# Pairs 7 and 8 transposed by DMA, early T work, and a DMA exchange in a fused attention and feed-forward kernel

## The chip, the cores and the metric

The kernel runs on one core of one Trainium2 chip. The metric is device microseconds of one execution; of several executions the median counts. A profile of one execution stands beside them. TensorE is PE in the profile (its weight loads PEld), VectorE is DVE, ScalarE is ACT, GpSimd is POOL, SyncE is SP.

## The reference

```python
def _attn_ref(q, k, v):                      # (8, 8, 1152, 64) each
    q_pool = q.reshape(B, H, S // 2, 2, D).mean(axis=3)      # 576 pooled queries a head
    scores = 1.0 / np.sqrt(D) * np.matmul(q_pool, k.transpose(0, 1, 3, 2))
    ...                                                      # softmax over the 1152 keys
    return np.matmul(attn, v)

def _moe_ref(x, w1, w2, w3, w_out):          # x (4608, 512): heads side by side
    a = x @ w1                               # (512, 1024)
    b = x @ w2
    h = a * b @ w3                           # (1024, 1024)
    return h @ w_out                         # (1024, 512)
```

The arithmetic is in 16-bit floats with sums in 32 bits; the result is 32-bit.

## The kernel before, in words

**Work.** The 64 heads are taken as 32 pairs; pair P is heads 2P and 2P+1, four pairs make a batch element. A pair's scores are 9 blocks of keys by 576 queries, and the two heads stand in the two 64-row halves of PE. The scores of all pairs form one stream that is cut in 324 chunks of 512 columns, so a pair is 10.1 chunks, and a boundary between pairs falls inside a chunk. `scores(c)` (L303) computes a chunk, `expo(c)` (L309) is ACT's exponential into the ring `er`, which holds 1.78 pairs. `attend(P, us)` (L312) multiplies the exponentials with the values (tile `po`; u is the head), `normalize` (L351) divides and sends the result, transposed by a DMA on SP, into `xT`. The last 64 queries of each head are the remainders: they go through `rems` by DMA into `xR` (the second half of the batches into a view of `wosb`), and `cross` (L378) copies each 64-row half of it into the other half.

**Feed-forward.** The product w3 @ w_out is formed once as `T16`: `w3_transpose(c)` (L476) transposes a block of w3 on PE (tile `w3t`, L493) and multiplies it with w_out (`pT`, L505), eight blocks in all. `add_batch(b)` then makes gates (`pg`, L546: x @ w1 and x @ w2 for 256 tokens, DVE copies one half and multiplies) and rows (`pp`, L570: gate times `T16`, then the store). w1 and w2 are loaded once and needed with their 64-row halves exchanged as well; `swap_halves` (L411) does that with a matmul by a swapped identity (`sw`, L419) and a copy.

**Preparation of a pair.** Keys and queries must be transposed. Pairs 1 to 8 (below `NPE`) take `prep_stage` and `prep_pe`: DVE copies the keys into `kc` and adds neighbouring queries into `qp` (`pool_q`, L138; for pairs 7 and 8 POOL makes the key copy), PE transposes (`t`, L271), DVE moves the results to `kT` and `qT` (L265, L261). From pair 9 on `prep_dma` (L158) does it: POOL copies the keys, adds the queries and copies the values, and two DMA transposes on SP (`turn_k` L168, `turn_q` L174) fill `kT` and `qT`. `turn_k` also has POOL wait for `kT` and then issue the loads of pair P + 5.

**The order.** The program is written out by a planner while it is built. It keeps a planned time for each PE half (`clock`), one for DVE (`vec`), and planned landings; its zero lies at the first scores, which start at 8.2 us in the profile. For each chunk it asks when the exponentials let the next scores go (`due`), and fills the time until then with one `step` of prepared work: first the queue `prep` (transposes), then `ffn` (T blocks, later the batches, in order). `LEAD` limits how far half 0 may run ahead of half 1 in `ffn`. `bursts` says at which chunk each pair's attention is multiplied (`BEHIND`, and `APART` for the distance of the two heads, J for both at once). `events`, `STAGE`, `PREP` and `turns` are in pairs of progress: `at = c * 512 / 5184`. `early` gives the chunk from which a T block may be queued. Each engine runs its instructions in the order written, so POOL's loads, copies and sums are one queue, and SP's transposes, exchanges and stores another.

Of the kernel before, what the change touches and what calls it, by code (L numbers as in the profile page):

```python
# [23 lines left out]
def kernel(  # L24
# [19 lines left out]
    SCL = 16.0  # L44
    NPE = 9
    T_SC, T_ACT, T_EXP, T_SEM, T_PV, LEAD = 0.225, 0.93, 1.05, 0.25, (1.78, 1.4), 2.53
    SCALE = 0.5 * float(D) ** -0.5
# [136 lines left out]
    def prep_stage(P):  # L184

        def copy_k(eng=nc.vector):
            eng.tensor_copy(out=new_kc(P).rearrange("p j u d -> p u j d"), in_=kst.pop(P))
# [12 lines left out]
        jobs.append((560, pool, LANDED[P][1]))  # L200
# [110 lines left out]

    def attend(P, us):  # L312

        pos = []
        for u in us:
            n = take()
            po = bank("po", n)
            pos.append((n, po, u))
            for j in range(NJ):
                for i in range(4):  # L320
                    r = ((P * NJ + j) * SQ) % RING + 128 * i
                    nc.tensor.matmul(  # L322
                        po[:, VW * i:VW * i + D + 1], er[:, u, r:r + 128],
                        vts[P % 4][:, u, j, 0:D + 1],
                        start=(j == 0 and i == 0), stop=(j == NJ - 1 and i == 3),
                        skip_group_check=True)
            if u == 0:
                for j in range(NJ):
# [6 lines left out]
        at = max(clock[0], clock[1], exp_done[last_chunk(P)] + T_SEM, V_COPIED.get(P, 0.0))  # L335
        b, hp = divmod(P, 4)
        for i, (n, po, u) in enumerate(pos):
            at += T_PV[u] - (0.2 if i else 0.0)
            give(n, normalize(P, u, po, 5 - u, at))
        clock[:] = [at] * 2  # L340
        if 0 in us and b % 2 == 1:
# [36 lines left out]
    def cross():  # L378

        b, _ = crossing.pop(0)  # L380
        x = xR[b // 4]
        k = (b // 2) % 2
        for h in range(2):
            nc.vector.tensor_copy(out=x[64 * h:64 * h + 64, 2 - 2 * h, :, k],  # L384
                                  in_=x[64 - 64 * h:128 - 64 * h, 1, :, k])
            vector(128, 0.0)
        if k == 1:
            crossed[b // 4][0] = vec + T_SEM

# [10 lines left out]

    def load_ffn(h):
        cols = slice(512 * h, 512 * h + 512)
        for dst, src in ((w1sb, moe_w1), (w2sb, moe_w2)):
            nc.gpsimd.dma_start(out=dst[:, 0, :, cols],
                                in_=src.rearrange("(c p) f -> p c f", p=128)[:, :, cols])
            swaps[h].extend((dst, c, cols) for c in range(NC))

# [68 lines left out]
    def w3_transpose(c):  # L476
# [3 lines left out]
        left = [2]  # L480
        landed = 13.0

# [12 lines left out]
        for h in range(2):  # L495
            add(prep, Block("w3t", NF, (h,), lambda t, at, h=h: out(t, at, h), FP16),
                0.0285, [[W3_LANDED[c // 2]]], emit)

# [107 lines left out]
    def step(h):  # L606
# [3 lines left out]
        for q in (prep[h], ffn[h]):  # L610
# [5 lines left out]
            q.pop(0)  # L616
            clock[h] += cost
            if q is ffn[h]:
# [19 lines left out]
    def last_rows(places, lhsT):  # L638
# [18 lines left out]
    NCHUNK = NP * PAIR // CH  # L657

    load_q(0)
    load_k(0)  # L660
# [3 lines left out]
        base=0, channel_multiplier=1, pattern=[[-1, 128]])  # L664
    load_v(0)
    load_k(1)
    load_q(1)
    load_w3(0)
    load_w(wosb, moe_w_out)
    load(2)  # L670
    load_w3(1)
    load(3)
    load_w3(2)
    nc.gpsimd.tensor_copy(out=swap[:, 0:64], in_=ident[:, 64:128])
# [3 lines left out]

    def last_chunk(P):
        return -(-(P + 1) * PAIR // CH) - 1  # L680

    def copy_v_later(P):
        if P < 4:
            jobs.append((280, lambda: copy_v(P), 0.0))
# [7 lines left out]
    LANDED = {1: (3.1, 4.3), 2: (13.4, 15.1), 3: (20.9, 22.7), 4: (28.9, 30.4), 5: (36.9, 38.1),  # L692
              6: (47.2, 48.8), 7: (57.9, 59.2), 8: (62.5, 64.6)}
# [12 lines left out]
    bursts = []  # L706
    for P in range(NP):
        at = last_chunk(P) + int(BEHIND[P])
        if APART[P] == "J":
            bursts.append((at, P, (1, 0)))  # L710
        else:
            bursts += [(at, P, (1,)), (at + int(APART[P]), P, (0,))]
    bursts.sort()

# [10 lines left out]
    while c < NCHUNK or bursts or ffn[0] or ffn[1]:  # L725
        h = 0 if clock[0] <= clock[1] else 1
        if crossing and crossing[0][1] < clock[h]:
            cross()
        if bursts and (c > bursts[0][0] or c == NCHUNK) and len(spare) >= len(bursts[0][2]) and (
                spare[len(bursts[0][2]) - 1][0] < clock[h]) and (  # L730
                fresh or c > bursts[0][0] + 1 or c == NCHUNK):
            attend(*bursts.pop(0)[1:])
# [4 lines left out]
        if c >= NCHUNK or due(c) > clock[h]:  # L737
# [5 lines left out]
            if bursts and c > bursts[0][0] - 1:  # L743
                keep = len(bursts[0][2])
            if not step(h):
# [13 lines left out]
        for i in range(2):  # L759
            clock[i] += T_SC  # L760
        expo(c)
# [3 lines left out]
        if jobs:  # L765
            n, job, landed = jobs.pop(0)
            job()
            vector(n, landed)
        if staged < NPE and at >= STAGE.get(
                staged, staged - (0.95 if staged < 4 else 1.3)):  # L770
# [55 lines left out]
```

## Time and profile before

| | |
|---|---|
| Runs | 418.47 us median of 3 (417.0 to 418.74) |
| Profiled execution | 415.05 us; span of its instructions 413.3 us |
| Granted clock of TensorE | 0.999 |
| PE, PEld busy | 395.1 us, 318.6 us |
| DVE, ACT, POOL busy | 224.4, 323.7, 191.7 us |
| DMA | 58.98 MB in 94217 packets |

Busy is time in which an engine had an instruction running. The ends of matmuls are modelled, so a high share of PE does not say that it ran at its peak. A stretch A:B is in microseconds from the start of the span. In a group's line the figures are busy time, mean nanoseconds of one instruction, and the idle time before them; in a DMA's line the last figure is the median time from issue to landing.

### The profile page before, as it was taken

The page shows a single profiled execution, that of the slowest core. Times are in us where ns is not written, and L with a number is a line of the kernel's source. Part 1 is how long each engine was busy: PE and PEld are TensorE (multiplying, and loading weights), DVE is VectorE, ACT ScalarE, POOL GpSimd, SP SyncE. Part 2 cuts the span into 40 slices and gives each one's busy share as a digit, 9 for nine tenths or more (in the row PEclk, how much of TensorE's full clock was granted, in tenths as well). Part 3 has the DMA queues.
Part 4 walks back from the last instruction along what each step waited for, and adds up shares of the span by engine and source line. Part 5 has one row for each costly group of instructions (what it writes and reads, how often), then busy time and mean ns, then how long its engine had stood idle before and what let it go on. Part 6 is the DMA issues. An engine that isn't in the chain of part 4 may idle for free.

```text
span 413.3 us, 16876 instructions
## 1 busy us (share of the span) xinstructions
PE 395.1 (96%) x7410; PEld 318.6 (77%) x7410; DVE 224.4 (54%) x585; ACT 323.7 (78%) x369; POOL 191.7 (46%) x209
## 2 busy tenths in 40 slices
PE   3699999999999999999999999999999999999996
PEld 1376765858778887887798986799688888998883
DVE  2256678585545564654465653477556644653530
ACT  3978889987989988879887889888888889834432
POOL 8243345770666666655654666665659400000000
PEclk9999999999999999999999999999999999999999
DMA  8999999998999999999999999999996324102004
GB/s 123 201 207 206 203 205 206 187 179 131 142 159 193 146 148 150 210 134 132 185 173 135 143 144 159 199 169 140 139 175 144 44 61 126 29 19 103 2 14 142
DMA packets 94217, 58.98 MB, mean 143 GB/s; under 512 B 64832, under 2 KB 84544, under 8 KB 94144
## 3 DMA queue, kind: packets, MB, share of 16 engines
q0 software_dynamic: 26528, 33.56, 52.3%
q1 hardware_dynamic: 67456, 24.22, 33.9%
q8 instruction: 58, 0.95, 1.0%
q10 hardware_dynamic: 160, 0.13, 0.1%
q14 instruction: 15, 0.12, 0.1%
HBM read 67.11 MB, written 9.44 MB: 185 GB/s over the span
## 4 chain that ended last, share of the span: by engine, by line
PE 92%; ACT 2%; DVE 2%; DMA 1%; issue 1%; POOL 0%; DVEq 0%; POOLq 0%
PE pg L546 30%; PE psc L303 19%; PE po L322 18%; PE pp L570 15%; PE pT L505 3%; PE po L331 3%; ACT er L309 2%; DMA kst<-in_k_dram 1%; PE sw L419 1%; PE t L271 1%; DVE wosb L384 1%; PE w3t L493 1%; DVE qp L145 0%; PE pp L644 0%; DVE asb L525 0%
## 5 line engine op out<-in xcount | busy, mean ns | idle before, releaser
L309 ACT ACTIVATE er<-psc 128x1024 f16<-128x1024 f32 x324 | 303.6, 1047 | 50.4 <-PE psc L303 50.1
L303 PE MATMUL psc<-qT,kT 64*128 64x512 f16 (+7 forms) x1152 | 128.8, 290 | 4.3 <-ACT er L309 3.8
L546 PE MATMUL pg<-xT,w2sb 64*128 64x256 f16 x1024 | 126.6, 269 | 0.2 <-issue 0.2
L546 PE MATMUL pg<-xT,w1sb 64*128 64x256 f16 x1024 | 124.7, 269 | 0.0
L546 PEld LDWEIGHTS <-w2sb 64*128 64x128 f16 x1152 | 94.9, 94 | 8.2 <-issue 1.9
L546 PEld LDWEIGHTS <-w1sb 64*128 64x128 f16 x1152 | 94.4, 94 | 7.2
L570 PE MATMUL pp<-T,gT 64*128 64x512 f16 (+1 forms) x552 | 94.3, 376 | 1.3 <-DVE gT L538 0.7
L303 PEld LDWEIGHTS <-kT 64*128 64x128 f16 x1152 | 63.1, 95 | 30.5 <-issue 16.0
L322 PEld LDWEIGHTS <-er 128*128 128x128 f16 x2304 | 73.7, 98 | 11.2 <-issue 8.7
L322 PE MATMUL po<-vt,er 128*128 128x65 f16 x2304 | 79.6, 194 | 0.1
L538 DVE TENSOR_TENSOR gT<-pg,asb 128x256 f16<-128x256 f32 x144 | 64.1, 445 | 19.2 <-ACT asb L522 14.1
L525 DVE COPY asb<-pg 128x256 f32<-128x256 f32 x116 | 49.0, 423 | 33.7 <-PE pg L546 32.7
L145 POOL TENSOR_TENSOR qp<-qst 64x1152 f16<-64x1152 f16 x23 | 54.9, 2388 | 1.0
L570 PEld LDWEIGHTS <-gT 64*128 64x128 f16 (+1 forms) x552 | 40.8, 94 | 14.5 <-issue 1.3
L355 DVE RECIPROCAL rz<-po 128x4 f32<-128x4 f32 x64 | 12.1, 188 | 71.0 <-PE po L331 37.2
L170 POOL COPY seen<-kT 1x1 f16<-1x1 f16 x19 | 3.4, 179 | 83.5 <-DMA kT<-kc 83.5
L154 POOL COPY vt<-vst 128x1152 f16<-128x1152 f16 x28 | 32.3, 1155 | 5.5 <-issue 4.8
L125 POOL DMA_DIRECT2D vst<-in_v_dram x32 | 23.4, 731 | 16.4 <-DMA kst<-in_k_dram 5.7
L118 POOL DMA_DIRECT2D kst<-in_k_dram x33 | 24.0, 729 | 10.6 <-issue 3.0
L358 DVE TENSOR_TENSOR xn<-po,rz 128x256 f16<-128x256 f32 x64 | 27.2, 425 | 2.4 <-DVE rz L355 0.2
L163 POOL COPY kc<-kst 128x1152 f16<-128x1152 f16 x23 | 27.0, 1173 | 0.0
L522 ACT COPY asb<-pg 128x256 f32<-128x256 f32 x28 | 10.4, 373 | 19.0 <-PE pg L546 15.3
(66 smaller groups left out, 255.4 us busy)
## 6 DMA issues: line engine op xcount, KB each, us to landing
qst<-in_q_dram POOLq DMA_DIRECT2D x32, 288.0 KB, 6.3
vst<-in_v_dram POOLq DMA_DIRECT2D x32, 288.0 KB, 7.8
kst<-in_k_dram POOLq DMA_DIRECT2D x31, 288.0 KB, 5.3
out_dram<-osb SPq DMA_DIRECT2D x32, 256.0 KB, 3.9
w3h<-in_moe_w_dram POOLq DMA_DIRECT2D x4, 512.0 KB, 15.0
wosb<-in_moe_w_out_dram POOLq DMA_DIRECT2D x1, 1024.0 KB, 13.4
xT<-xn SPq DMA_TRANSPOSE x64, 5.4
w1sb<-in_moe_w_dram POOLq DMA_DIRECT2D x2, 512.0 KB, 14.8
```

Source lines behind the costliest of these rows:

```text
L118: nc.gpsimd.dma_start(out=kst[P][:, :, js[0]:js[1], :], in_=k[b, h0:h0 + 2].rearrange("u (p j) d -> p u j d", j=NJ)[:, :, js[0]:js[1], :])
L145: (eng or nc.vector).tensor_tensor(out=qps[pp][r].rearrange("p c u d -> p u c d"), in0=src[:, :, :, 0, :], in1=src[:, :, :, 1, :], op=ALU.add)
L154: (eng or nc.vector).tensor_copy(out=vts[P % 4][:, :, :, 0:D], in_=vst.pop(P))
L163: nc.gpsimd.tensor_copy(out=kc.rearrange("p j u d -> p u j d"), in_=kst.pop(P))
L303: nc.tensor.matmul(t[:, u, o:o + ln], kT[P][s, j, :], qv[s, f0:f0 + ln], start=True, stop=True)
L309: nc.scalar.activation(out=er[:, :, r:r + CH], in_=psc.pop(c), func=AF.Exp, bias=0.0, scale=SCALE)
L322: nc.tensor.matmul(po[:, VW * i:VW * i + D + 1], er[:, u, r:r + 128], vts[P % 4][:, u, j, 0:D + 1], start=(j == 0 and i == 0), stop=(j == ...
L358: nc.vector.tensor_tensor(out=xn, in0=acc[:, 0:4, 0:D], in1=rz[:, 0:4].to_broadcast([128, 4, D]), op=ALU.mult)
L525: nc.vector.tensor_copy(out=a, in_=t[:, 0:n])
L538: nc.vector.tensor_mul(out=g, in0=b, in1=a)
L546: nc.tensor.matmul(t[:, n * w:n * w + n], (w1sb, w2sb)[w][s, (m + h) % 2, m // 2, fs], x(h, s, m), start=start, stop=stop, skip_group_chec ...
L570: nc.tensor.matmul(t, g(s, i), T16[s, i, :], start=start, stop=stop, skip_group_check=True)
```

## The change

- `NPE` goes from 9 to 7: pairs 7 and 8 take `prep_dma`. Their value copies stay separate events, their turns come at P - 1.6 and P - 1.35, and they issue no loads. `PREP` has them at 4.7 and 5.75; a pair is only prepared after the pair before it (pair 6 at 4.94). The loads of pairs 9, 10 and 11 move from 4.75, 5.0, 5.95 to 5.2, 5.9, 6.1.
- `early` goes from chunks (14, 14, 19, 21, 26, 30, 39, 40) to (7, 7, 17, 18, 31, 41, 41, 43), and up to five blocks may be open instead of four.
- `cross` uses two DMAs on SP instead of two DVE copies; the plan lets the remainder's gates wait 6 us more, and delays the first exchange of each two by 6 us.
- The order of the loads is written as a list, and the planned landings `LANDS` are a formula over it. The order up to pair 8 is the same as before. The halves of w1 and w2 become swappable one by one, from planned 42.3 and 62.6 instead of 46.0 and 70.4.
- `LEAD` goes from 2.53 to 3.79; until the planned time `COLD` = 9 matmuls count double in the plan; the times in `STAGE` and `PREP`, `BEHIND` and `APART` are new.
- A burst may be cut into slices, and a T block may be transposed by DMA; `SLICES`, `W3_DMA` and the letter D leave both unused.

```diff
-    NPE = 9
-    T_SC, T_ACT, T_EXP, T_SEM, T_PV, LEAD = 0.225, 0.93, 1.05, 0.25, (1.78, 1.4), 2.53
+    NPE = 7
+    T_SC, T_ACT, T_EXP, T_SEM, T_PV, LEAD = 0.225, 0.93, 1.05, 0.25, (1.78, 1.4), 3.79
+    COLD = 9.0
...
         pool_q(P, nc.gpsimd)
-        copy_v(P, nc.gpsimd)
+        if P > 8:
+            copy_v(P, nc.gpsimd)
...
-            if P + 5 <= NP:
+            if P > 8 and P + 5 <= NP:
...
-        turns.extend([(P - 1.45, turn_k), (P - 1.2, turn_q)])
+        turns.extend([(P - (1.45 if P > 8 else 1.6), turn_k), (P - (1.2 if P > 8 else 1.35), turn_q)])
...
-        if P == 7:
-            copy_k(nc.gpsimd)
-            kc_done[P] = LANDED[P][0] + 9.0
-        elif P == 8:
-            copy_k(nc.gpsimd)
-            kc_done[P] = LANDED[P][0] + 10.0
-        else:
-            jobs.append((280, copy_k, LANDED[P][0]))
+        jobs.append((280, copy_k, LANDED[P][0]))
...
-                crossing.append((b, landed))
+                crossing.append((b, landed + (6.0 if b % 4 == 1 else 0.0)))
...
         for h in range(2):
-            nc.vector.tensor_copy(out=x[64 * h:64 * h + 64, 2 - 2 * h, :, k],
-                                  in_=x[64 - 64 * h:128 - 64 * h, 1, :, k])
-            vector(128, 0.0)
+            nc.sync.dma_start(out=x[64 * h:64 * h + 64, 2 - 2 * h, :, k],
+                              in_=x[64 - 64 * h:128 - 64 * h, 1, :, k])
         if k == 1:
-            crossed[b // 4][0] = vec + T_SEM
+            crossed[b // 4][0] = max(clock) + 6.0
...
-        return bool(swaps[half]) and max(clock) > WEIGHTS[half] and len(spare) >= free and (
+        if not swaps[half]:
+            return False
+        landed = LANDS[("f" if swaps[half][0][0] is w1sb else "g") + str(half)] + T_SEM
+        return max(clock) > max(WEIGHTS[half], landed) and len(spare) >= free and (
             spare[0][0] < min(clock))
...
-        landed = 13.0
+        landed = LANDS["wo"]
...
-            clock[h] += cost
+            clock[h] += cost * (2 if clock[h] < COLD else 1)
...
+    ORDER = ("v0 k1 q1 w0 wo k2 q2 v1 w1 k3 q3 v2 w2 k4 q4 v3 w3 k5 q5 v4 "
+             "f0 g0 k6 q6 v5 f1 g1 k7 q7 v6 k8 q8 v7").split()
+    mb, LANDS = 0.0, {}
+    for n in ORDER:
+        mb += {"w": 1.05, "f": 1.05, "g": 1.05}.get(n[0], 0.59) * (2 if n == "wo" else 1)
+        LANDS[n] = 0.3 + 2.38 * mb if mb < 5.51 else 13.4 + 2.74 * (mb - 5.51)
...
-    early = list(zip((14, 14, 19, 21, 26, 30, 39, 40), range(8)))
-    STAGE = {1: 0.39, 2: 1.2, 3: 2.0, 4: 3.02, 5: 4.2, 6: 4.94, 7: 5.15, 8: 6.95}
-    W3_LANDED = (7.1, 19.0, 27.6, 35.1)
+    early = list(zip((7, 7, 17, 18, 31, 41, 41, 43), range(8)))
+    STAGE = {1: 0.39, 2: 1.26, 3: 2.02, 4: 2.85, 5: 3.5, 6: 4.32, 7: 5.15, 8: 6.95}
+    W3_LANDED = [LANDS["w%d" % i] for i in range(4)]
...
-    PREP = {1: 0.67, 2: 1.38, 3: 1.9, 4: 3.2, 5: 4.43, 6: 5.41, 7: 5.72, 8: 7.49}
+    PREP = {1: -0.42, 2: 0.76, 3: 2.34, 4: 2.61, 5: 2.95, 6: 4.94, 7: 4.7, 8: 5.75}
     events = sorted(
-        [(0.0, 4, load), (0.0, 3, load_w3), (0.4, 5, load), (0.4, 0, load_ffn), (1.2, 6, load),
-         (1.2, 1, load_ffn), (2.3, 7, load), (4.0, 8, load), (4.75, 9, load), (5.0, 10, load),
-         (5.95, 11, load), (6.95, 12, load), (7.05, 13, load)]
-        + list(zip((1.97, 2.59, 3.9, 4.35, 5.1, 5.4, 6.1, 7.0), range(1, NPE),
-                   [copy_v_later] * NPE)), key=lambda e: e[0])
-    WEIGHTS = (46.0, 70.4)
+        list(zip((0.0,) * 4 + (0.4,) * 5 + (1.2,) * 5 + (2.3,) * 3 + (4.0,) * 3, ORDER[13:],
+                 [issue] * 20))
+        + [(5.2, 9, load), (5.9, 10, load), (6.1, 11, load), (6.95, 12, load), (7.05, 13, load)]
+        + list(zip((1.55, 2.95, 3.21, 4.35, 5.1, 5.4, 6.1, 7.0), range(1, 9),
+                   [copy_v_later] * 8)), key=lambda e: e[0])
+    WEIGHTS = (42.3, 62.6)
...
-    BEHIND = "22123222333244224212222222232434"
-    APART = "35J2144JJ42JJ1J2JJJJJ41J4J14J3JJ"
+    BEHIND = "22422222333442422221223242212432"
+    APART = "33344434J2J4JJJ221JJ36JJ3J3JJ4JJ"
...
-        elif early and c >= early[0][0] and len(w3T) < 4:
+        elif early and c >= early[0][0] and len(w3T) < 5 and (
+                early[0][1] < W3_DMA or W3_LANDED[early[0][1] // 2] < clock[0] + 1.0):
```

More of the change, by code (lines that the diff above doesn't have):

```diff
@@ L310, in expo, with attend @@
                              bias=0.0, scale=SCALE)
-    def attend(P, us):
+    held = {}
+    def attend(P, us, js=range(NJ)):
         pos = []
         for u in us:
-            n = take()
-            po = bank("po", n)
+            if js[0] == 0:
+                n = take()
+                held[P, u] = n, bank("po", n)
+            n, po = held[P, u]
             pos.append((n, po, u))
-            for j in range(NJ):
+            for j in js:
                 for i in range(4):
@@ L327, in attend @@
             if u == 0:
-                for j in range(NJ):
+                for j in js:
                     r = ((P * NJ + j) * SQ) % RING + 512
@@ L334, in attend @@
                             skip_group_check=True)
-        at = max(clock[0], clock[1], exp_done[last_chunk(P)] + T_SEM, V_COPIED.get(P, 0.0))
+        at = max(clock[0], clock[1], exp_done[last_chunk(P, js[-1])] + T_SEM,
+                 V_COPIED.get(P, 0.0))
         b, hp = divmod(P, 4)
+        cold = 0.9 * len(js) / NJ if at < COLD else 0.0
         for i, (n, po, u) in enumerate(pos):
-            at += T_PV[u] - (0.2 if i else 0.0)
-            give(n, normalize(P, u, po, 5 - u, at))
+            at += (T_PV[u] - 0.26) * len(js) / NJ + (0.06 if i else 0.26) + cold
+            if js[-1] == NJ - 1:
+                give(n, normalize(P, u, po, 5 - u, at))
         clock[:] = [at] * 2
+        if js[-1] < NJ - 1:
+            return
         if 0 in us and b % 2 == 1:
@@ L399, in load_w, with load_part, load_f, load_g @@
         nc.gpsimd.dma_start(out=dst, in_=src.rearrange("(c p) f -> p c f", p=128))
-    def load_ffn(h):
+    def load_part(h, dst, src):
         cols = slice(512 * h, 512 * h + 512)
[L403 to L406, printed above, removed]
+        nc.gpsimd.dma_start(out=dst[:, 0, :, cols],
+                            in_=src.rearrange("(c p) f -> p c f", p=128)[:, :, cols])
+        swaps[h].extend((dst, c, cols) for c in range(NC))
+    def load_f(h):
+        load_part(h, w1sb, moe_w1)
+    def load_g(h):
+        load_part(h, w2sb, moe_w2)
     swaps = ([], [])
@@ L494, in emit @@
                                 w3h[c // 2][s, c % 2, 128 * n:128 * n + 128], ident[s, s])
-        for h in range(2):
-            add(prep, Block("w3t", NF, (h,), lambda t, at, h=h: out(t, at, h), FP16),
-                0.0285, [[W3_LANDED[c // 2]]], emit)
+        if c < W3_DMA:
+            for h in range(2):
+                add(prep, Block("w3t", NF, (h,), lambda t, at, h=h: out(t, at, h), FP16),
+                    0.0285, [[W3_LANDED[c // 2]]], emit)
+        else:
+            nc.sync.dma_start_transpose(out=w3T[c], in_=w3h[c // 2][:, c % 2])
+            ready[0] = max(clock[0], W3_LANDED[c // 2]) + 8.0 + 1.5 * (c % 2)
         def copy(t, at):
@@ L657, with issue @@
     NCHUNK = NP * PAIR // CH
+    SLICES = (1, 1, 1, 1)
+    W3_DMA = 8
+    ORDER = ("v0 k1 q1 w0 wo k2 q2 v1 w1 k3 q3 v2 w2 k4 q4 v3 w3 k5 q5 v4 "
[4 more added lines that the diff above has]
+        LANDS[n] = 0.3 + 2.38 * mb if mb < 5.51 else 13.4 + 2.74 * (mb - 5.51)
+    def issue(n):
+        if n == "wo":
+            load_w(wosb, moe_w_out)
+        else:
+            {"k": load_k, "q": load_q, "v": load_v, "w": load_w3, "f": load_f, "g": load_g}[n[0]](
+                int(n[1]))
     load_q(0)
@@ L664 @@
         base=0, channel_multiplier=1, pattern=[[-1, 128]])
[L665 to L673, printed above, removed]
+    for n in ORDER[:13]:
+        issue(n)
     nc.gpsimd.tensor_copy(out=swap[:, 0:64], in_=ident[:, 64:128])
@@ L710 @@
             bursts.append((at, P, (1, 0)))
-        else:
-            bursts += [(at, P, (1,)), (at + int(APART[P]), P, (0,))]
-    bursts.sort()
+        elif APART[P] == "D":
+            bursts += [(last_chunk(P, js[-1]) + int(BEHIND[P]) - 1, P, (1, 0), js)
+                       for js in (range(0, 3), range(3, 6), range(6, 9))]
+        else:
+            for n, u in enumerate((1, 0)):
+                m = SLICES[P] if P < len(SLICES) else 1
+                bursts += [(at + n * int(APART[P]) + i, P, (u,), range(NJ * i // m, NJ * (i + 1) // m))
+                           for i in range(m)]
+    bursts.sort(key=lambda b: b[:2] + (-b[2][0],))
     def due(c):
@@ L728 @@
             cross()
-        if bursts and (c > bursts[0][0] or c == NCHUNK) and len(spare) >= len(bursts[0][2]) and (
-                spare[len(bursts[0][2]) - 1][0] < clock[h]) and (
-                fresh or c > bursts[0][0] + 1 or c == NCHUNK):
+        new = len(bursts[0][2]) if bursts and (len(bursts[0]) == 3 or bursts[0][3][0] == 0) else 0
+        full = c == NCHUNK or bursts and (c + 1) * CH > bursts[0][1] * PAIR + RING
+        if bursts and (full or c > bursts[0][0]) and len(spare) >= new and (
+                new == 0 or spare[new - 1][0] < clock[h]) and (
+                full or fresh or c > bursts[0][0] + 1):
             attend(*bursts.pop(0)[1:])
@@ L743 @@
             if bursts and c > bursts[0][0] - 1:
-                keep = len(bursts[0][2])
+                keep = len(bursts[0][2]) if len(bursts[0]) == 3 or bursts[0][3][0] == 0 else 0
             if not step(h):
@@ L759 @@
         for i in range(2):
-            clock[i] += T_SC
+            clock[i] += T_SC * (2 if clock[i] < COLD else 1)
         expo(c)
@@ L765 @@
         if jobs:
-            n, job, landed = jobs.pop(0)
+            n, job, landed, *pair = jobs.pop(0)
             job()
             vector(n, landed)
+            for P in pair:
+                V_COPIED[P] = vec + T_SEM
         if staged < NPE and at >= STAGE.get(
```

9 lines of the change are left out of this document (4 added, 5 removed).

## The prediction

> **What bounds the kernel now.** I read the page's busy shares and slices first, then busy time by stage, the waits, and the DMA issues with the landing times behind them.
>
> ```profile
> PE 395.1 (96%) x7410; PEld 318.6 (77%) x7410; DVE 224.4 (54%) x585; ACT 323.7 (78%) x369; POOL 191.7 (46%) x209
> PEld 1376765858778887887798986799688888998883
> DMA  8999999998999999999999999999996324102004
> ```
>
> PE shows 96%, but ends of matmuls are modelled, so a half-empty PE still reads as busy. The weight loads (PEld) say more: 1 to 7 tenths in the first nine slices, 8 to 9 later. DMA is full for nine slices. Busy time by stage (columns: stretch, its length, PE, PEld, DVE, ACT, POOL, clock, DMA share):
>
> ```profile
> 8.00:20.00 12.00, 8.58 (x78) 4.20 (x79) 3.91 (x9) 10.60 (x12) 4.38 (x7) 1.00 1.16 195
> 20.00:30.00 10.00, 9.27 (x204) 7.01 (x202) 5.57 (x16) 7.91 (x9) 3.87 (x7) 1.00 1.17 209
> 30.00:60.00 30.00, 29.85 (x605) 21.17 (x604) 20.11 (x53) 25.85 (x29) 12.24 (x17) 1.00 1.19 204
> 60.00:72.00 12.00, 11.85 (x213) 6.96 (x211) 10.53 (x24) 10.82 (x13) 5.81 (x8) 1.00 1.20 206
> 82.00:95.00 13.00, 12.44 (x231) 7.94 (x231) 10.81 (x24) 10.38 (x13) 7.99 (x7) 1.00 1.27 184
> 100.00:370.00 270.00, 267.41 (x5244) 225.54 (x5242) 150.04 (x398) 226.11 (x245) 142.61 (x140) 1.00 0.89 139
> ```
>
> To price the difference I took each matmul's spacing where nothing waits, from PE's start times in the trace (256-column row-half 53 ns, 512-column 107, po 33, 64-column transpose 14), and called the rest of each stretch lost. Work: 362.5 us. Lost: 7.9 before the first scores at 8.2, 8.4 until 20, 3.7 in 20-30, 3.2 in 30-60, 2.6 in 60-72, 0.7 in 72-82, 3.6 in 82-100, 14.5 in 100-370 (0.54 per 10 us), 2.3 after. That makes 409.4, the last matmul; the stores end at 413.3 and the execution takes 415.05. From 370 on PE has only feed-forward work, so a backlog always exists: PE work removed, or lost time filled, comes off the end one for one. ACT is the limit only until about 20 us. The profiled execution is 3.4 us under the median of the runs, 418.47; I take my difference from the median.
>
> **The change, part by part.** (A) Pairs 7 and 8 leave PE. In the PE timeline 18 key transposes take 0.26 us and 9 query ones 0.27, so 0.53 a pair where they stand alone, 0.38 at 14 ns where the other half has work: two pairs 0.8 to 1.06. I take **-0.9**.
>
> (B) T earlier. The first transposes of w3 stood at 23.2 us and the first pT at 28.0, though the first w3 block landed at 15.0 and w_out at 20.1. The new thresholds (chunk 7 for both first blocks) and the planned landings (7.0 and 12.0, plus 8.2 for the first scores) put them at 15.2 and 20.2. One pT block is 16 x 107 ns = 1.7 us, so 20-30, with 3.7 lost, can take most of two; the 32 transposes (0.45 us) go into a stretch where PE waits for the exponentials. At most 20-30 falls to the steady 0.5 and 0.45 comes from before: 3.6. At least nothing: blocks 4 to 7 are not sooner (chunks 31, 41, 41, 43 against 26, 30, 39, 40), and 35 to 51 us may lack filler. There ACT could make up: it was busy 25.85 of 30 us in 30-60, and scores that run ahead carry their attention work with them. I take **-2.0**, nearer the upper end because it is the row of the idle stretch itself.
>
> (C) The start of the feed-forward part. In 60-72 and 72-100 the loss is 6.9; at 0.54 per 10 us it would be 2.2, so 4.7 is in reach. DVE is what is full there:
>
> ```profile
> L425 DVE CAST w2sb<-sw 128x512 f16<-128x512 f32 x3 | 2.0, 684 | 0.0
> L425 DVE CAST w1sb<-sw 128x512 f16<-128x512 f32 x3 | 2.0, 682 | 0.0
> L145 DVE TENSOR_TENSOR qp<-qst 64x1152 f16<-64x1152 f16 x1 | 1.9, 1875 | 0.0
> ```
>
> These are DVE's groups in 82-95: copies of the half-swapped weights and pair 8's query sum, ahead of the gates. The change lets the swaps begin at planned 43.0 and 62.6 instead of 46.0 and 70.4 (the weights landed at 50.2 and 60.0, that is 42.0 and 51.8), and takes from DVE two query sums (0.76 and 1.88 us) and six evictions of 0.45: 5.3 us. The swaps' own 12 casts stay (8.2 us). Bounds 0 and -4.0; I take half of what is in reach, **-2.3**.
>
> (D) Exchange by DMA. DVE's first pair of copies into wosb took 1.52 and 1.14 us at 288, where the other half's took 0.29, and PE lost 0.91 us at 291.6 waiting for the gate product behind them:
>
> ```profile
> L384 DVE COPY wosb<-wosb x4: 289/714/1524, 287.9 to 374.5; 64x512 f16<-64x512 f16 x4
> L384 DVE COPY xR<-xR x4: 285/288/289, 111.4 to 200.3; 64x512 f16<-64x512 f16 x4
> ```
>
> Off the path it costs eight SP DMAs of 64 KB. Behind them on SP stand xT, kT and qT transposes; the plan sends the first of each two 6 us after landing, so SP should not wait. The remainder's gates come 6 us later; batch 3's or 7's own 16 gates (16 x 16 x 53 ns = 13.6 us) stand in front. If that cover went, up to 6 us. **-0.7** (bounds -0.9 and +0.5, SP standing for a late landing).
> The Trainium skill ("SBUF — State Buffer", SBUF: two separate sides) says that DVE in a two-port mode and GpSimd take a shared port whole, one blocking the other. The trace agrees: POOL's query sum ran to 289.3, and the blocked DVE copy ended at 289.5. By that rule two more query sums on POOL can block DVE for 2 x 2.4 us, and the sum would be 4.8 us worse if all of it reached PE.
>
> (E) The new spacing of attention bursts, the lead 3.79 for 2.53 and the cold factor reorder everything. Pairs split in two bursts go from 16 to 18; a burst begins with 0.17 to 0.20 us lost in the PE gaps: **+0.4**. Some 40 bursts account for 8 of the 14.5 us lost in 100-370; half of the other 6.5 is my bound both ways, 3. Slices of one, the w3 DMA path (limit 8 of 8 blocks) and "D" bursts are not reached: nothing.
>
> (G) What is added: POOL copies k7, then sums q7, before it issues the load of pair 9.
>
> ```profile
> 60.55 0.71 POOL L118 DMA_DIRECT2D kst<-in_k_dram  x1 [0.64 <-DVE qp L145]
> 67.11 0.71 POOL L118 DMA_DIRECT2D kst<-in_k_dram  x1 [0.30 <-DVE kc L187]
> 88.46 2.75 POOL L145 TENSOR_TENSOR qp<-qst 64x1152 f16<-64x1152 f16 x1
> ```
>
> k7 landed at 65.6; copy 1.2 and sum 2.4 end at 69.2, so pair 9's load (here 60.55) goes out at 69.3, pair 10's (67.11) near 76. Pair 9 is touched by POOL only near 87, so the delay is hidden by 5 us or more. The transposes are not so free:
>
> ```profile
> xT<-xn SPq DMA_TRANSPOSE x64, 5.4
> kT<-kc SPq DMA_TRANSPOSE x23, 7.1
> qT<-qp SPq DMA_TRANSPOSE x23, 5.4
> ```
>
> While loads run (55 to 90 us) one xT took 7.4 to 8.2 us instead of 2.3 late in the run: first packet 3.5 us after issue, then some 75 packets per half microsecond, one for each load packet; with no loads 400. A kT is 1152 packets, a qT 576, two xT and the remainder 640. Pair 7's, issued at 67 and 69, with one xT and remainder (2112 packets), land near 79 if the loads pause while POOL is busy, near 84 if not. Chunk 70 needs them at 85 in the old pace, near 80 if attention runs 5 us ahead. Pair 8's 2368 packets need 15.8 us at that rate, to 95, against 98 or 93. PE is in order: a late operand stops gates and scores alike. Bounds 0 and 8; I take **+1.0**, near zero, since the old pace leaves them on time.
> The Trainium skill ("DMA: Bandwidth & Descriptors", Queues, rings and completion order) says that each DMA engine goes round robin between its queues by packet. The one-for-one packets agree, and the rule speaks against this change; what it would make of the time is the first rival.
>
> Sum: -0.9 - 2.0 - 2.3 - 0.7 + 0.4 + 1.0 = -4.5, so 410.5 for a profiled execution and **414.0** as median.
>
> **Rivals.** (1) Slower: loads never pause, packets alternate throughout. Pair 7's queries land at 84 and pair 8's at 100; PE stands at chunk 70 for 4.4 us and at chunk 81 for 4. Instead of 1.0 that is 8.4: 421.4. It decides the sign once these stalls pass 1.0 + 4.5 + 2.1 = 7.6 us. For it: the packet rates. Against: POOL holds back the very loads that compete. (2) No change: T early only moves the idle time to 35-51, and the swaps stay bound by DVE's casts; without B and C the sum is -0.2: 418.3. For it: lost time in 30-60 is already small, so there the filler was used. (3) More: B 3.6, C 4.0, D 0.9, no stall: 418.47 - 0.9 - 3.6 - 4.0 - 0.9 + 0.4 = 409.5. For it: chunk 47, which frees pair 3, could come at 54 instead of 59.5 us if ACT ran at 0.93 us a chunk. (4) The change does not do as it says: pair 7 cannot be prepared at 4.7, since pair 6 comes first at 4.94; it falls to chunk 52, load 9 to 53. The order holds by one chunk, so I give this nothing of its own.
>
> **How the numbers follow.** Forecast 0.43, rival 1 0.20, rival 2 0.17, rival 3 0.20. A measurement of this kernel can tell about 0.5%, 2.1 us, from no change: below 416.4 is faster (forecast and rival 3, 0.63), above 420.6 slower (0.20), between 0.17. The range goes from 407.5 (rival 3 with 2 us of E's bound) to 421.5 (rival 1). The forecast's own range is 411 to 416.4.
>
> **What would show it.** First pT near 20.2 and no loss above 2 in 20-30 (B); second-half swaps done before 82 and first gates before 70 (C); no L271 group of pairs 7 and 8, eight more DMAs and no stretched copy at 288 (A, D). PE waiting on DMA kT or qT near chunks 70 and 81 beyond 2 us makes the forecast wrong towards rival 1; a first gate still near 72 towards rival 2.

## The result and the profile after

| | before | after |
|---|---|---|
| Runs measured together | 417.74 us median of 4 | 430.66 us median of 4 (429.65 to 432.71) |
| Ratio, 95% interval | | 1.032 (1.027 to 1.037) |
| Profiled execution | 415.05, span 413.3 us | 429.65, span 427.8 us |
| Granted clock | 0.999 | 0.975 |

The change makes the kernel 3.2% slower, 13 us, where 4.5 us less had been forecast. Some executions of any of these kernels run some per cent longer than the rest; ratios compare only the others, on both sides, and in three experiments (pair 7's time put right, turns earlier on SP, the second with the chain of preparation broken) the profiled execution was such a long one, so that no profile of these is read.

The page of the kernel before, its chain of waits and the group of the scores:

```profile
PE 92%; ACT 2%; DVE 2%; DMA 1%; issue 1%; POOL 0%; DVEq 0%; POOLq 0%
L303 PE MATMUL psc<-qT,kT 64*128 64x512 f16 (+7 forms) x1152 | 128.8, 290 | 4.3 <-ACT er L309 3.8
```

The page of the kernel after, its busy times, slices, chain of waits and the group of the scores:

```profile
PE 397.5 (93%) x7356; PEld 317.5 (74%) x7356; DVE 212.9 (50%) x569; ACT 324.3 (76%) x369; POOL 196.0 (46%) x211
PEld 1467767653487897888788997788778987898883
PEclk9999999968599999999999999999999999999999
PE 78%; DMA 14%; ACT 2%; POOL 2%; issue 1%; SPq 1%; DVE 1%; POOLq 0%; DVEq 0%
L298 PE MATMUL psc<-qT,kT 64*128 64x512 f16 (+7 forms) x1152 | 131.1, 291 | 16.5 <-DMA qT<-qp 13.4
```

Nearly all of it stands in these lines. PE has 54 instructions fewer, the transposes of pairs 7 and 8, and DVE is relieved by 11.5 us. But PEld falls to 5, 3 and 4 tenths in slices nine to eleven (86 to 118 us), the clock falls in the same slices, and the scores wait 13.4 us for `qT` from a DMA, a wait that the page of before does not have. Busy time by stage, three of the stretches that were shown of before (columns as there), and behind them short ones around the first long wait:

```profile
20.00:30.00 10.00, 10.00 (x207) 6.89 (x204) 5.08 (x16) 9.15 (x11) 3.91 (x7) 1.00 1.16 205
60.00:72.00 12.00, 12.00 (x216) 8.51 (x214) 5.64 (x16) 10.63 (x12) 7.83 (x8) 1.00 1.21 202
82.00:95.00 13.00, 9.98 (x125) 5.68 (x120) 5.26 (x12) 7.31 (x9) 5.33 (x7) 0.74 1.25 176
```

```profile
84.00:86.00 2.00, 0.00 (x0) 0.00 (x0) 0.24 (x1) 0.14 (x1) 0.60 (x1) 0.95 1.26 168
86.00:88.00 2.00, 1.27 (x14) 1.06 (x15) 0.00 (x0) 0.94 (x1) 0.00 (x0) 0.50 1.17 187
88.00:90.00 2.00, 2.00 (x12) 0.49 (x7) 0.86 (x3) 1.11 (x2) 0.00 (x0) 0.50 1.33 135
...
94.00:96.00 2.00, 2.00 (x63) 1.68 (x57) 1.32 (x3) 1.69 (x2) 0.85 (x2) 1.00 1.76 143
```

The early stretches are better: PE is busy for all of 20-30 instead of 9.27 us (PEld is not higher, 6.89 against 7.01), and DVE in 60-72 fell from 10.53 to 5.64 us. The loss begins at 83.5 us. PE has nothing for 3.3 us, and when it starts again its clock is 0.50 until about 92.6 us: a gate matmul takes 417 ns instead of 269. The same comes again at 100.5: 10.4 us without work, then 0.50 until about 116.5. (Waits of PE in this text are counted from where the last matmul's spacing ends; the idle times in the profile's rows go by modelled ends and are 0.2 to 0.3 us shorter.)

Lost PE time, counted as in the prediction and summed from the start (us):

| up to | before | after | difference |
|---|---|---|---|
| 20 us | 16.3 | 15.8 | -0.5 |
| 40 us | 21.2 | 19.1 | -2.1 |
| 60 us | 23.2 | 23.2 | 0.0 |
| 80 us | 26.4 | 26.3 | -0.1 |
| 120 us | 31.6 | 46.7 | +15.1 |

So the new start, early T work with it, did win 2.1 us by 40 us, lost them again by 60, and everything that the change costs falls between 80 and 120. Of the 20.4 us lost there (before: 5.2), 13.7 are the two waits and 5.9 the two stretches of 6 us at half clock behind them (3.1 and 2.8 in the counting by microsecond).

Where the waits come from is seen in the pieces of the chain of waits of after, in order of time (start, duration, what):

```profile
74.42 2.28 POOL qp L146
76.70 12.82 DMA kst<-in_k_dram
...
89.60 21.12 DMA qT<-qp
```

and in SP's timeline of after (start, time to issue):

```profile
72.33 1.37 SPq L176 DMA_TRANSPOSE qT<-qp  x1
74.86 3.59 SPq L367 DMA_TRANSPOSE xT<-xn  x1
78.56 2.12 SPq L170 DMA_TRANSPOSE kT<-kc  x1
81.26 6.97 SPq L367 DMA_TRANSPOSE xT<-xn  x1
88.32 1.18 SPq L346 DMA_TRANSPOSE xR<-rems  x1
89.60 5.23 SPq L176 DMA_TRANSPOSE qT<-qp  x1
```

Pair 7's queries, issued at 72.3, landed at 86.7. Pair 8's were summed at 76.7 but issued only at 89.6: in SP's order the keys, an xT and a remainder stand ahead of them, and that xT alone took 7.0 us to issue (an issue takes 1.2 us where the queue is free). They landed at 110.7, 21 us later. And POOL's timeline of after shows that the loads which compete never paused for long:

```profile
76.70 0.74 POOL L119 DMA_DIRECT2D kst<-in_k_dram  x1
78.74 0.72 POOL L119 DMA_DIRECT2D kst<-in_k_dram  x1
82.90 0.72 POOL L119 DMA_DIRECT2D kst<-in_k_dram  x1
91.86 0.72 POOL L119 DMA_DIRECT2D kst<-in_k_dram  x1
```

Pair 9's loads went out at 70.1, these are pairs 10 to 13. Packets started in each 4 us of the trace of after, counted by queue:

```
us             80   84   88   92   96  100  104  108
transposes    601  428  389  457  406  445  873 1688
loads         477  459  390  452  413  446  341   44
```

From 84 to 104 us about one transpose packet goes for each load packet, 97 to 115 a us each, although most load packets have 1152 bytes and those of the transposes 256; when the loads end, 1688 transpose packets go in 4 us.

### The profile page after: what moved, and what is told of

Same layout as the page of the kernel before. It is cut to its first block, busy times and chain, and to the rows that moved or that the text cites. A ratio compares the mean times of both kernels' runs of the same rounds, so it can differ in the third digit from the quotient of the medians.

```text
span 427.8 us, 16765 instructions
## 1 busy us (share of the span) xinstructions
PE 397.5 (93%) x7356; PEld 317.5 (74%) x7356; DVE 212.9 (50%) x569; ACT 324.3 (76%) x369; POOL 196.0 (46%) x211
## 4 chain that ended last, share of the span: by engine, by line
PE 78%; DMA 14%; ACT 2%; POOL 2%; issue 1%; SPq 1%; DVE 1%; POOLq 0%; DVEq 0%
PE pg L561 26%; PE po L321 16%; PE psc L298 16%; PE pp L585 15%; DMA kst<-in_k_dram 7%; DMA qT<-qp 6%; PE po L330 3%; ACT er L304 2%; PE pT L520 2%; DMA qst<-in_q_dram 1%; POOL qp L146 1%; SPq L170 1%; POOL kc L164 1%; PE pp L659 0%; PE t L266 0%
## 5 line engine op out<-in xcount | busy, mean ns | idle before, releaser
L298 PE MATMUL psc<-qT,kT 64*128 64x512 f16 (+7 forms) x1152 | 131.1, 291 | 16.5 <-DMA qT<-qp 13.4
L561 PEld LDWEIGHTS <-w1sb 64*128 64x128 f16 x1152 | 93.1, 95 | 9.2 <-issue 1.0
L561 PEld LDWEIGHTS <-w2sb 64*128 64x128 f16 x1152 | 93.7, 95 | 7.4 <-issue 0.9
L146 POOL TENSOR_TENSOR qp<-qst 64x1152 f16<-64x1152 f16 x25 | 59.1, 2364 | 1.1
L585 PEld LDWEIGHTS <-gT 64*128 64x128 f16 (+1 forms) x552 | 39.3, 94 | 14.3 <-issue 0.4
L172 POOL COPY seen<-kT 1x1 f16<-1x1 f16 x19 | 3.5, 182 | 89.6 <-DMA kT<-kc 89.6
L126 POOL DMA_DIRECT2D vst<-in_v_dram x32 | 23.2, 725 | 18.2 <-DMA kst<-in_k_dram 7.5
L164 POOL COPY kc<-kst 128x1152 f16<-128x1152 f16 x25 | 29.0, 1160 | 4.8 <-DMA kst<-in_k_dram 4.1
L520 PE MATMUL pT<-wosb,w3T 64*128 64x512 f16 x128 | 26.4, 376 | 0.0
```

The lines of the kernel that those rows point to most:

```text
L146: (eng or nc.vector).tensor_tensor(out=qps[pp][r].rearrange("p c u d -> p u c d"), in0=src[:, :, :, 0, :], in1=src[:, :, :, 1, :], op=ALU.add)
L298: nc.tensor.matmul(t[:, u, o:o + ln], kT[P][s, j, :], qv[s, f0:f0 + ln], start=True, stop=True)
L520: nc.tensor.matmul(t, w3T[c][s, n, :], wosb[s, n, :], start=start, stop=stop, skip_group_check=True)
L561: nc.tensor.matmul(t[:, n * w:n * w + n], (w1sb, w2sb)[w][s, (m + h) % 2, m // 2, fs], x(h, s, m), start=start, stop=stop, skip_group_chec ...
L585: nc.tensor.matmul(t, g(s, i), T16[s, i, :], start=start, stop=stop, skip_group_check=True)
```

## The experiments

The first theory, rival 1 of the prediction: the loads of pairs 9 to 13 share the DMA engines with the transposes of pairs 7 and 8, packet by packet, and PE stands for the queries. Against it: the order of issue on SP; the new order of bursts and T blocks; GpSimd's added work.

**Pairs 7 and 8 back on PE** in the changed kernel, with the loads as in before.

```diff
-    NPE = 7
+    NPE = 9
...
-        + [(5.2, 9, load), (5.9, 10, load), (6.1, 11, load), ...
+        + [(4.75, 9, load), (5.0, 10, load), (5.95, 11, load), ...
```

> The changed kernel with pairs 7 and 8 prepared as before (PE transposes, loads of 9, 10, 11 at the old places), all else as changed. Theory Q (the transposes of pairs 7 and 8 land late because their packets share the DMA engines one for one with the loads): the 13.4 us in which PE stood for qT goes, 430.7 to 416 to 419. Theory S (SP's or POOL's own queue makes them late, the loads don't matter): the same here. Theory O (the new order of bursts, lead and T blocks is what costs): 427 or more.

Measured: ratio 1.015 (1.007 to 1.023), profiled 423.01. That is above the 416 to 419 us that the first two theories gave and below the third's. No PE wait for pairs 7 and 8 and no fall of the clock near 100, but 6.8 us lost in 60-80 (before: 3.2). DVE's timeline of this kernel says why: the planned time 5.15 for pair 7's queries, which the changed kernel never uses, has DVE stand for their landing, and evictions and normalisations stand behind it.

```profile
67.86 0.76 DVE L146 TENSOR_TENSOR qp<-qst 64x1152 f16<-64x1152 f16 x1 [3.22 <-DMA qst<-in_q_dram]
```

PE also stands for the queries of later pairs, five times between 200 and 330 us, as its waits show; whether that follows from the first stall is not shown.

```profile
PE psc L305 <- DMA qT<-qp: 5.0, 5, 1.8
```

So the same with that time put right.

```diff
-    STAGE = {..., 6: 4.32, 7: 5.15, 8: 6.95}
+    STAGE = {..., 6: 4.32, 7: 5.65, 8: 6.95}
```

> As e1 (the changed kernel, pairs 7 and 8 on PE), with pair 7 staged at 5.65 instead of 5.15 pairs of progress. In e1 DVE stood 3.2 us at 64.6 for the queries of pair 7, and every later pair's transposes landed with no slack. If that one stall started it (theory: preparing pair 10 and after is a chain with a period as long as a pair's attention, so lateness stays), this gives 417 to 420 and under 1.5 us of waits on qT and kT. If the new order itself loses it, 422 to 425.

Measured: 1.0047 (1.0003 to 1.0091). The median, 418.4 us, lies in the 417 to 420 that the first theory gave; its waits cannot be read. This is the whole change without its DMA transposes for pairs 7 and 8: about 2 us slower than before, not 4.6 faster. The other 2.7%, 11 us, belong to the two pairs.

**Later loads** in the changed kernel; nothing but GpSimd's queue moves.

```diff
-        + [(5.2, 9, load), (5.9, 10, load), (6.1, 11, load), (6.95, 12, load), (7.05, 13, load)]
+        + [(6.7, 9, load), (6.75, 10, load), (7.3, 11, load), (7.4, 12, load), (7.5, 13, load)]
```

> The changed kernel with only the loads of pairs 9 to 13 held back on POOL (to 6.7, 6.75, 7.3, 7.4, 7.5 pairs of progress), so that the transposes of pairs 7 and 8 meet fewer loads; PE, DVE, ACT and SP have the same instructions in the same order. Theory Q: qT of pair 8 lands before 98, PE's wait on qT falls from 13.4 to under 4 us, 417 to 422. Theory S: the wait stays above 10 us, 428 to 432. Theory O: 427 or more as well.

Measured: 1.016 (1.010 to 1.023), profiled 425.37. The waits view of this kernel, against 13.4 us in all and 10.2 at most:

```profile
PE psc L298 <- DMA qT<-qp: 8.8, 3, 5.2
```

The time lies between the ranges of theory Q (417 to 422) and of the other two. Pair 7's wait is gone, pair 8's is 2.9 instead of 10.4 us. But 5.4 us come up at 128.6 for pair 10. The loads of pairs 11 to 14 now go out close together, from 100.9 on: GpSimd stood 3.6 us before it could send out the last of them at 113.3, and copied pair 10's keys only then. Their transpose, issued at 115.2, ran beside the loads of pairs 13 and 14, which landed by 119.9 and 126.1. The cost follows the loads.

**Half the load packets** in the changed kernel: only the first head of these pairs is loaded, and GpSimd reads it twice.

```diff
+        us = slice(0, 1 if 9 <= P <= 13 else 2)
...
-                out=kst[P][:, :, js[0]:js[1], :],
+                out=kst[P][:, us, js[0]:js[1], :],
```

(Likewise the source, queries and values.)

> Changed kernel whose loads of pairs 9 to 13 (of the values 8 to 12) bring only the first of the two heads; GpSimd's copies and sums read that head twice, so every instruction but these loads is as long as before, and the attention of these pairs is left half computed from the other head. The transposes, their order on SP and the moment each load goes out stay. Theory (load packets hold the transposes up one for one): between 80 and 104 us about 1300 load packets go instead of 2600, pair 8's queries land 10 us or more earlier, near 97 to 100 instead of 110.7; of the 13.7 us that PE stood for pairs 7 and 8 at most 3 remain, and with the clock that stays up the time is 417 to 420.5 us. Rival (SP's order: the queries' transpose of pair 8 is issued too late, behind an xT): issue still near 88, the wait at pair 8 stays above 5 us, 424 to 428 us. Third (POOL's copies too late): no change from 430.7.

Measured: 1.0009 (0.996 to 1.006), profiled 416.08. The waits view has no line of PE for `kT` or `qT`; its page:

```profile
PEclk9999999999999999999999999999999999999999
PE 91%; DMA 4%; issue 2%; POOL 1%; SPq 1%; ACT 1%; DVE 0%; DVEq 0%; POOLq 0%
```

and SP's timeline for pair 8:

```profile
78.49 2.43 SPq L180 DMA_TRANSPOSE kT<-kc  x1
83.25 1.17 SPq L377 DMA_TRANSPOSE xT<-xn  x1
84.52 1.18 SPq L356 DMA_TRANSPOSE xR<-rems  x1
85.79 1.24 SPq L186 DMA_TRANSPOSE qT<-qp  x1
```

The order on SP is the same and the keys are issued at the same time (the last load, pair 13's, goes out at 84.7 instead of 91.9), but the xT takes 1.2 us to issue instead of 7.0, the queries go out 3.8 us earlier and land at 97.2 instead of 110.7. PE still lost 2.4 us up to 97.2, the moment of that landing; the profile names no releaser for it. This settles the cause: the loads, which also made SP's queue back up. Half the loads is half the packets and half the bytes alike; that the share goes by packets rests on the count above. The range expected was 417 to 420.5; the median was 416.9.

**Turns earlier on SP** in the changed kernel.

```diff
-        turns.extend([(P - (... else 1.6), turn_k), (P - (... else 1.35), turn_q)])
+        turns.extend([(P - (... else 2.0), turn_k), (P - (... else 1.95), turn_q)])
```

> Changed kernel with one edit: the transposes of pairs 7 and 8 have their turn on SP at P-2.0 and P-1.95 instead of P-1.6 and P-1.35, so that they stand ahead of the xT transposes of that time. Theory (packets: while loads are in flight the transposes' queue gets one packet for each load packet, some 111 a us, and pairs 7 and 8 with the xT and remainders of that stretch are some 4100): pair 8's queries land near 100 to 104, PE still stands 2 to 6 us for them, 421 to 426 us. Rival (the order on SP: the queries' transpose stood at 89.6 behind an xT whose issue took 7 us): it goes out near 77, lands by 95, no wait above 1 us at pair 8, 417 to 420 us. Third (the loads' issue order alone): no change from 430.7.

Inconclusive: a single time can be compared, 423.45 us, inside the packet theory's range and above the rival's, with no interval.

**Pairs 7 and 8 by DMA alone**, in the kernel before, with the loads of pairs 9 to 11 at 5.6, 5.9, 6.1.

```diff
-    NPE = 9
+    NPE = 7
...
+        full = bursts and (c + 1) * CH > bursts[0][1] * PAIR + RING
...
```

The same edit without the line `full`, run first, gave no result.

> The kernel before with only pairs 7 and 8 by DMA and POOL (turns at P - 1.6 and P - 1.35, loads of 9, 10, 11 at 5.6, 5.9, 6.1; a burst that the ring is waiting for goes at once, as in the change). Theory Q (packets of the transposes share the DMA engines one for one with the loads): PE waits 5 to 14 us on qT of pairs 7, 8 or the next, 422 to 431. Theory O (the cost lies in the new order of bursts and T blocks): under 2 us of such waits, 415 to 419.

Measured: 1.018 (1.009 to 1.027), profiled 426.89. PE waits 0.55, 0.54 and 2.86 us for the queries of pairs 7, 8 and 9, and 4.0 us at 118.2 for something else, of which DVE's timeline of this kernel shows the cause:

```profile
113.72 4.21 DVE L385 COPY xR<-xR 64x512 f16<-64x512 f16 x2 [4.87 <-DMA xR<-rems]
```

The part slows the old order too. The time is in theory Q's range, but the waits for queries, 4.0 us together, are below its 5. Here another late operand comes in, the remainders' transpose, for which DVE stands 4.9 us, and then its two exchange copies (0.29 us each when free) take 4.2 us together and end at 117.9, where POOL's value copy ended at 117.8.

**The exchange by DMA alone**, in the kernel before.

```diff
-            nc.vector.tensor_copy(out=x[64 * h:64 * h + 64, 2 - 2 * h, :, k], ...
+            nc.sync.dma_start(out=x[64 * h:64 * h + 64, 2 - 2 * h, :, k], ...
```

> The kernel before with only the remainders' exchange by DMA. By the prediction's term 0.7 us less than before, so no change that can be told: 415 to 419; the stretched copies at 288 are gone and PE's 0.9 us there with them.

Measured: 0.998 (0.994 to 1.002), profiled 414.71; lost in 290-300: 0.36 us against 1.24. No change can be told in the time, as expected; the loss at that place is gone.

**Early T work alone**, in the kernel before, with the change's thresholds and five open blocks; then with the DMA exchange as well; then with that exchange and the last four thresholds left as they were. All three also have the line `full` and w_out planned at 12.0.

```diff
-    early = list(zip((14, 14, 19, 21, 26, 30, 39, 40), range(8)))
+    early = list(zip((7, 7, 17, 18, 31, 41, 41, 43), range(8)))    # first and second
+    early = list(zip((7, 7, 17, 18, 26, 30, 39, 40), range(8)))    # third
```

> The kernel before with only the early T thresholds (7, 7, 17, 18, 31, 41, 41, 43), five open blocks, w_out planned at 12.0. Prediction's term B: 2 us less than before, 414 to 416. Rival 2 of the prediction (the idle time only moves to 35-51 us): 416 to 418, 2 us less lost before 40 us and 2 us more in 40-60.

> Kernel before with the change's thresholds of the T blocks (7, 7, 17, 18, 31, 41, 41, 43) and five open blocks, as in the earlier run, and now the exchange of the remainders by DMA. Theory (the DVE copies of the exchange, which take up to 2 us each while GpSimd works, cost the earlier run 4.4 us by two stalls of PE): no PE wait behind them, 417.5 to 419.5 us; the rest above before is the 40 to 60 us stretch, where filler is short (4 us lost in 20 against 2). Rival (the stalls move with the order of the bursts and come back at another place): 421 to 423.

> The kernel before with the first four T thresholds early (7, 7, 17, 18), the last four where they were (26, 30, 39, 40), and the exchange by DMA. If filler is what 40-60 us lacked, the 2 us gained before 40 are still given back there, since the sum of T work is the same: 415.5 to 417.5. If the thresholds 31, 41, 41, 43 were at fault: 413 to 415.

Measured: 1.012 (1.003 to 1.021), 1.004 (1.0003 to 1.007) and 0.998 (0.994 to 1.001). The first, 422.6 us, is above both ranges expected; the other two, 419.1 and 416.3, are in their theory's. Lost PE time, summed:

| up to | before | early T | + exchange | late four back | changed, 7 and 8 on PE, late four back |
|---|---|---|---|---|---|
| 40 us | 21.2 | 19.0 | 20.0 | 18.9 | 18.2 |
| 60 us | 23.2 | 25.0 | 25.9 | 22.8 | 23.9 |

All win 1 to 3 us by 40 us; by 60 they have given back most of it, or more. That is not the whole story: by the same count the third kernel is some 2 us ahead of before again at 120 us, and no longer at 370, with a wait of 1.8 us for the queries of a late pair at 309 between. In the first, DVE's exchange copies cost again; its timeline, and PE's:

```profile
116.49 3.60 DVE L384 COPY xR<-xR 64x512 f16<-64x512 f16 x2
120.12 0.15 DVE L462 COPY handed<-pp 1x1 f32<-1x1 f32 x1
```

```profile
120.33 0.61 PE L570 MATMUL pp<-T,gT 64*128 64x512 f16 x4 [2.37 <-DVE handed L462]
```

With the exchange by DMA this wait and one of 1.75 us at 300.8 are gone, as its theory had it.

**Late thresholds back in the changed kernel** (pairs 7 and 8 on PE, 5.65):

> Changed kernel with pairs 7 and 8 on PE (pair 7's queries staged half a pair later, 5.65, as in the run before) and the last four T thresholds back at 26, 30, 39, 40 instead of 31, 41, 41, 43. Theory (the thresholds 41 and 43 leave 40 to 60 us short of filler, 4 us lost against 2): 1.5 to 2.5 us below the same kernel with the later thresholds, 415.5 to 417.5 us, and less than 3 us lost in 40 to 60. Rival (the gap is ACT's, whatever the filler): 418 to 419.5 us.

Measured: 0.9995 (0.995 to 1.004). The interval overlaps that of the same kernel with the later thresholds (1.0003 to 1.0091), so a gain is not shown. The time fits the theory, but its mechanism does not: 5.7 us were lost in 40-60, not less than 3 (last column above).

**The chain of preparation broken**, in the kernel before and in the third early kernel: GpSimd copies the next pair before it waits for this pair's transpose.

```diff
...
-            0.65 if prepped < 4 else 0.9 if prepped < NPE else 1.9))
+            0.65 if prepped < 4 else 0.9 if prepped < NPE else 2.45 if prepped > 9 else 1.9))
```

> Kernel before, with one edit: for pairs from 10 on GpSimd copies the keys and sums the queries of the next pair before it waits for the keys' transpose of this pair (preparation planned at P-2.45 instead of P-1.9, the value copy as a turn of its own at P-1.9). Theory (preparation is a chain: a transpose's landing lets GpSimd begin the next copy, 3.7 us, whose transpose takes 7.0, about a pair's 11.1 us): the slack between the landing of a pair's queries and PE's need, 1.5 to 5.7 us in before, rises to 6 or more from pair 11 on. There is little to win by it in the kernel before, since PE waits for none of these there: 415.5 to 418.5 us. Rival (slack set by DMA or GpSimd's own load): slack stays below 5, time 418 to 421.

> Kernel before with the thresholds of the T blocks 7, 7, 17, 18, 26, 30, 39, 40, the exchange of the remainders by DMA, and the chain of preparation broken as in the run beside it. Theory: the 1.8 us that PE lost waiting for pair 27's queries without the broken chain are gone, the early T blocks' 1 to 2 us stay won: 413.5 to 415.5 us. Rival (early T work is given back whatever the preparation does, because PE has filler enough and ACT sets 40 to 60 us): 416 to 418.

Measured: 0.997 (0.992 to 1.002) and 0.996 (0.992 to 1.0005). In the first the copies were ready 6.5 to 14 us before the transpose was issued (without the edit mostly under 1), yet the slack of pairs 11 to 27 stayed between 1.1 and 5.7 us. My theory fell: the copies do not hold the issue. What does may be the planned turn on SP, P - 1.45; no run moved it for these pairs. The second run's gain of 1 to 2 us is not shown either. No version was shown faster than the kernel before; the four nearest to it, at 0.996 to 0.998, have intervals that reach 1.

## Why the prediction was wrong

**G, the late transposes, is the step that failed**: +1.0 was taken between bounds of 0 and 8. The waits came to 13.7 us and the half clock behind them to 5.9, and PE waiting over 2 us for qT near chunks 70 and 81 is the sign that the prediction named. That packets alternate one for one was read rightly from the trace. What failed is, first, the choice between the ends: "POOL holds back the very loads that compete" and "the old pace leaves them on time". POOL held pair 9's load until 70.1, forecast 69.3, and pair 10's until 76.7, forecast 76; but pairs 11 to 13 followed at 78.7, 82.9 and 91.9, so load packets were in flight throughout the two transposes. Second, the rate: "75 packets per half microsecond", 150 a us, is near the peak of single transposes; sustained it was 97 to 115. At that rate pair 8's 2368 packets need 21 to 24 us, not 15.8. Third, the half clock behind a wait was priced at nothing. Without the two pairs the change is at 1.0047, with them at 1.032: their price is 11.4 us, A's gain included (less than the 19.6 us of waits and half clock, since before lost 5.2 in the same stretch; the remaining 3 us are not accounted for).

**Rival 1 was right in its mechanism and short in its price**, 8.4 us for the two waits. The waits are 3.3 and 10.4. Both its landings were too early: 84 forecast, 86.7 measured for pair 7; 100 and 110.7 for pair 8. Missing were the rate, the late issue of pair 8's queries, 12.9 us after their sum (SP's order, and a queue that backs up and holds SP itself: with half the loads they went out 3.8 us sooner), and the half clock. By the count of 256-byte packets in order of issue pair 8's queries would have been through near 106; why they landed some 4 us later is left open. The count fits the Trainium skill's round robin by packet ("DMA: Bandwidth & Descriptors", Queues, rings and completion order), which the prediction cited: 445 transposes against 446 loads in 100-104 (that the trace's packets are that page's is not shown).

**B, early T**: first pT at 21.8 (forecast 20.2, before 28.0), 2.3 us lost in 20-30 (the sign was at most 2, before 3.7), and -2.1 us by 40 us against -2.0 forecast. All of it was given back by 60, as rival 2 had it. The columns above show that neither the thresholds nor the exchange mends this. That work taken ahead is missing later, in a stretch that attention paces, is the likely reason and not shown; what holds attention in 40-60 was not isolated. The late thresholds make it worse, 25.9 against 22.8 us lost.

**C, start of the feed-forward part**: DVE was relieved and the first half's swaps were done at 60.4 instead of 67.5, but the second half's, begun at 74.0 instead of 82.4, ended at 93.5 (before 91.7; 90.0 with half the load packets), not before 82, and the first gate came at 70.0 against 71.9. At 80 us, ahead of the first wait, nothing of the 2.3 us was there (26.3 against 26.4 lost); in 60-100 the kernel with half the loads lost 7.2 us, 2.4 of them its wait, against 6.9 in before, so without waits up to 2 us of C may be there (an estimate).

**D, exchange by DMA**: alone -0.8 us by the ratio, forecast -0.7, but the interval, -2.3 to +0.8, holds zero too, so the time does not show it; the 0.9 us less lost in 290-300 do. No stretched copy is left at 288. Its bound was too narrow: in other orders the same DVE copies cost PE 2.6 us, and 4.0 together with a late transpose ahead of them, so the DMA's worth depends on when POOL works.

**A**: the 54 PE instructions are gone; their 0.9 us was not measured by itself. **E** cannot be separated: B, C, D and E together were forecast at -4.6 us and measured at +2.0 (0.1 to 3.8).

## What to carry to other kernels

Price a transfer that is moved onto a busy DMA system by what else is in flight until it lands, not by its median latency, and count the loads that follow the delayed one. A late operand can cost more than its wait: in the changed kernel each long wait of PE brought some 3 us more at half clock. Filling an early idle stretch pays only if the stretch that loses the work has other work to do; sum the lost time to the end of the next stage before booking it.

## What the runs showed of the hardware

- The granted clock fell to 0.50 with PE waits of 3.3 and 10.4 us in the changed kernel, and stayed there for some 6 us of work behind each. It also fell with the wait of 2.6 us in the kernel with early T work (0.50 in 121-123 us, 0.66 in 123-125), with those of 2.9 and 5.4 us in the kernel with later loads (0.66 in 102-106; 0.50 in 130-132, 0.99 in 132-136), and with pairs 7 and 8 back on PE after only 1.7 us without work up to 69.2 (0.50 in 70-72). It did not fall with the wait of 2.4 us up to 97.2 in the run with half the loads, nor with the 2.86 us for pair 9 at 111.4 in the kernel before with pairs 7 and 8 by DMA. So in these runs the length of a wait alone does not tell. The Trainium skill ("TensorE: Matmul & The Clock Gate", Part 1: The HAM clock gate) gives half rate after an idle window of about 3.4 us, free-running; these runs agree with half rate, but waits shorter than that were enough three times.
- SP's issue of one DMA transpose took up to 7.0 us while loads were in flight (81.3 us in the changed kernel), and 1.2 us for the same xT with half the loads.
- Two DVE copies of 0.29 us took 3.6 and 4.2 us together while POOL summed or copied; in the early kernel they ended at 120.09, POOL's sum at 119.95. That agrees with the shared port of the Trainium skill ("SBUF — State Buffer", SBUF: two separate sides), which the prediction weighed.
